# Sums of mm2's products gathered in one bank, some elementwise work on other engines, loads by single pages, and a new list of steps

## The chip, the cores and the metric

The kernel runs on one core of a Trainium2 chip. The metric is the device time of one execution in microseconds (us); the median of three runs of the kernel before is 296.47 us (296.28 to 297.04). PE is TensorE (its matmuls; PEld its weight loads), DVE is VectorE, ACT is ScalarE, POOL is GpSimd, SP is the engine that issues most DMAs.

## What is computed

The reference is a decayed linear attention followed by a two-layer MLP:

```python
batch, n_heads, seq, head_dim = (8, 8, 576, 64)
scores = scale * q @ k.T                      # per batch and head
gamma = 1.0 - 2.0 ** (-5.0 - np.arange(H))
Dmat = np.where(rel >= 0, gamma ** rel, 0.0)  # rel = row - column
x = ((scores * Dmat) @ v).transpose(0, 2, 1, 3).reshape(B * S, H * D)   # 4608 x 512
h = x @ w_in                                  # 512 x 2048
g = 0.5 * h * (1.0 + np.tanh(c * (h + 0.044715 * h * h * h)))
out = g @ w_out                               # 2048 x 512, float32
```

## The kernel before

The work of the attention is cut into 40 units, five per batch: four of 128 rows and a tail of 64. The decay is put into q and v (a product with a table, `dec` or `decw`), so that inside a unit a 0/1 mask is enough, and a running state (the sum of k^T v, two half-steps per unit) carries what lies before. Four pairs of units at the start (0 and 1, 2 and 3, 5 and 6, 7 and 8) are done as "wide" units of 256 rows. The MLP runs over nine blocks of 512 tokens: mm1 (x @ w_in), gelu, mm2 (g @ w_out). From block 1 on, mm2 is done per pair of 128-token tiles with seven products in place of eight: both operands are cut into 2x2 blocks, sums of blocks are formed on both sides, and the results are assembled from the seven products. For mm1 the same is done in the blocks 6 to 8.

Nothing is scheduled by the chip or by a planner at build time. The string `ORDER` is a list of steps written out by hand, and each engine gets its instructions in the order of this list. A step has a letter, its indices, and often the engine (`a` ACT, `g` POOL, `v` DVE):

- `L,u,n` loads q, k or v (n = 0, 1, 2) of unit u on SP; `I,g` and `J,g` load an eighth of w_in or w_out, by DMAs that POOL issues
- `q`, `k`, `v`: multiply or cast the loaded page to fp16; `t`/`D`: transpose by PE or DMA; `y`: copy a transpose out of its bank
- `X`, `Y,u,part`, `R` (wide units) and `B,u,w`: the matmuls of state, scores and result; `m`: the mask (L691, or L644 for wide units); `a`: add to the state (L711, L713); `o`: decay of the state; `z`: state to fp16; `x`: result to xT
- `N,t,f,half` and `M,t,f`: mm1 for two rows of 128 outputs and half of a block's tokens, or for one row and all tokens (L757); `F`, `G`: its gelu (L765); `O,t,n`: mm2 of block 0 (L783); `K,n`: n filler matmuls on the identity (L1003)
- `T` and `H,t,pr,i`: sums of blocks of w_out and of gelu's result (`tsum`, `ssum`, L817); `W,t,pr,i`: product i of mm2 (L860), eight matmuls of 256 columns; `V,t,pr,i`: the i-th step of assembly (L267, L269 or L817)
- `U` and `s,t,i`: sums of blocks of w_in and of x (they lie in the space of the tile `pages`); `A`, `l`, `f`: products (L957), assembly and gelu of mm1 in blocks 6 to 8
- `S`, `Q`: store

The products of mm2 go to two banks per pair, taken from a ring of two. Before, bank 0 is taken at product 1 and bank 1 at product 6. Products 1 and 2 share the left half of bank 0, 7 and 4 its right half, 6 has the left half of bank 1, 5 and 3 share the right one. Assembly copies product 1, adds product 6 and later sums in SBUF tiles `u1` to `u3`, and writes the blocks of `ost`, with five adds on DVE and two copies per pair.

The tile `pages` holds 21 pages of 256 KB for loads. Before, unit u takes three pages together, by u modulo 7 (modulo 3 from unit 31 on, when nine pages are left and the rest holds the sums `U` and `s`).

Of the kernel before, what the change touches and what calls it, by code (L numbers as in the profile page):

```python
# [17 lines left out]
L,0,1 Z,1,v L,0,0 I,2,g L,0,2 L,2,1 L,2,0 Z,2,g q,0 k,0,g I,7,g K,4 K,4 K,4 K,3 K,4 t,0,q,h L,2,2  # L18
L,4,1 c t,0,k,h I,1,g v,0,v X,0 y,0,k,v I,0,g I,3,g a,0,1 y,0,q,v Z,3,v k,2,g K,4 K,1 Y,0,1 t,2,k,o
m,0,1 z,0,1,a I,6,g K,4 Y,0,0 a,1,1 q,2 L,4,0 K,4 t,2,q,h m,0,0 y,2,k,a y,2,q,v I,4,g K,1 R,0 I,5,g  # L20
x,0 Y,2,1 L,5,0 x,1 i,4,v K,3 N,0,2,0 N,0,0,0 g o,1,1 m,2,1 L,5,1 Z,4,g v,2,v F,0,2,0 N,0,12,0 Y,2,0
F,0,0,0 z,1,1,v N,0,4,0 L,5,2 X,2 k,4,g Z,5,v q,4 F,0,12,0 F,0,4,0 t,4,k,o a,2,1 t,4,q,o a,3,1
y,4,q,a N,0,8,0 L,4,2 z,2,1,g L,9,1 N,0,10,0 F,0,8,0 k,5,g m,2,0 L,7,1 R,2 F,0,10,0 y,4,k,v B,4,-1
q,5 x,3 x,2 N,0,14,0 L,7,0 t,5,q,o N,0,0,1 L,7,2 J,1,g F,0,14,0 N,0,6,0 y,5,q,v J,3,g t,5,k,o
F,0,0,1 m,4 j,1,v J,0,g L,9,0 v,5,v J,2,g L,9,2 F,0,6,0 N,0,8,1 L,10,0 N,0,12,1 k,7,v X,5 y,5,k,a
F,0,8,1 z,3,1,g F,0,12,1 v,4,v Y,5,0 a,5,1 m,5,0 a,6,1 N,0,4,1 N,0,6,1 F,0,4,1 q,7 F,0,6,1 t,7,k,o
y,7,k,a N,0,2,1 J,5,g J,4,g N,0,14,1 F,0,2,1 J,6,g L,10,2 B,-1,4 F,0,14,1 x,4 Y,5,1 t,7,q,h y,7,q,a
J,7,g m,5,1 N,0,10,1 v,7,v F,0,10,1 z,5,1,g R,5 x,5 Y,7,0 o,6,1 x,6 O,0,0 O,0,4 q,10,g L,11,1
N,1,4,0 O,0,5 N,1,14,0 F,1,4,0 m,7,0 N,1,2,0 L,12,2 O,0,1 X,7 Y,7,1 F,1,14,0 F,1,2,0 L,15,1 k,9,a
O,0,6 O,0,2 N,1,10,0 F,1,10,0 q,9,g O,0,3 L,11,2 N,1,6,0 D,9 F,1,6,0 m,7,1 Z,0,g k,11,a a,7,1 O,0,7  # L30
e,0,0,v a,8,1 z,6,1,v O,0,12 T,1,0,v N,1,0,0 e,0,1,a F,1,0,0 z,8,1,g z,7,1,v N,1,8,0 O,0,13 L,10,1
N,1,12,0 R,7 B,9,-1 H,1,0,3,v v,10,v F,1,8,0 x,8 O,0,8 L,11,0 L,12,1 O,0,14 j,5,v F,1,12,0 v,11,v
T,1,1,v q,11 k,10,g x,7 O,0,15 N,1,6,1 H,1,0,1,v L,12,0 D,10 N,1,8,1 O,0,9 F,1,6,1 T,2,0,v v,9,v
O,0,10 e,0,3,a T,3,0,v S,0,0 N,1,14,1 F,1,8,1 H,1,0,2,v m,9 L,14,1 B,10,9 k,12,a D,11 T,2,1,v O,0,11
a,10,0 a,10,1 e,0,2,v N,1,12,1 L,13,2 F,1,14,1 L,13,0 x,9 N,1,10,1 m,10 F,1,12,1 T,3,1,v z,10,0,g
B,11,10 q,12,g W,1,0,1 S,0,3 v,13,v a,11,0 V,1,0,0,a a,11,1 x,10 v,12,v W,1,0,6 L,14,0 F,1,10,1
N,1,2,1 o,11,1 q,13,g F,1,2,1 T,4,0,v D,12 W,1,0,2 L,16,1 V,1,0,1,v N,1,4,1 N,1,0,1 S,0,2 V,1,0,2,a
z,11,0,v F,1,4,1 z,10,1,g j,2,v m,11 S,0,1 N,2,0,0 B,12,11 q,14 a,12,0 H,1,0,4,v k,15,g F,1,0,1
F,2,0,0 W,1,0,7 L,15,0 L,14,2 N,2,8,0 T,4,1,v N,2,4,0 V,1,0,3,v H,1,1,1,v L,13,1 z,12,0,g x,11
k,16,g H,1,1,2,v W,1,0,4 W,1,0,5 F,2,8,0 L,17,0 a,12,1 N,2,6,0 L,17,1 V,1,0,5,v L,19,0 F,2,4,0  # L40
k,13,g D,13 V,1,0,4,v F,2,6,0 m,12 N,2,14,0 v,14,v F,2,14,0 W,1,1,1 z,11,1,g V,1,1,0,a W,1,0,3
V,1,0,6,v L,16,0 N,2,10,0 F,2,10,0 k,14,g W,1,1,6 V,1,1,1,v N,2,12,0 z,12,1,v L,16,2 B,13,12 x,12
L,15,2 v,15,g D,14 q,15 W,1,1,2 H,1,1,3,v m,13 N,2,2,1 V,1,1,2,a W,1,1,7 F,2,12,0 N,2,2,0 V,1,1,3,v
k,17,a W,1,1,4 W,1,1,5 a,13,0 a,13,1 S,1,0 z,13,0,a q,19 q,17 q,16 F,2,2,1 S,1,1 D,15 L,17,2 F,2,2,0
L,18,0 N,2,8,1 B,14,13 N,2,12,1 L,20,0 F,2,8,1 V,1,1,5,v F,2,12,1 N,2,6,1 V,1,1,4,v W,2,0,1 x,13
N,2,10,1 F,2,6,1 m,14 H,2,0,1,v H,2,0,2,v z,13,1,v N,2,0,1 D,16 V,2,0,0,a L,24,1 B,15,14 H,1,1,4,v
a,15,0 L,18,2 H,2,0,3,v W,1,1,3 a,15,1 F,2,0,1 m,15 V,1,1,6,v q,18,g v,17,v F,2,10,1 N,2,4,1
N,2,14,1 L,18,1 L,19,1 x,14 v,16,g F,2,14,1 W,2,0,2 z,15,0,g B,16,15 W,2,0,6 F,2,4,1 x,15 k,19,g
a,16,0 N,3,8,0 V,2,0,1,v V,2,0,2,a a,16,1 F,3,8,0 o,16,1 z,16,0,v m,16 W,2,0,7 D,17 V,2,0,3,v L,23,1
v,18,g N,3,10,0 k,18,g F,3,10,0 L,24,0 L,20,1 N,3,4,0 F,3,4,0 z,15,1,g W,2,0,4 z,16,1,v B,17,16  # L50
L,21,0 N,3,0,0 q,20 V,2,0,5,v a,17,0 L,25,1 L,19,2 D,18 H,2,0,4,v L,20,2 S,1,2 W,2,0,5 N,3,12,0
W,2,1,1 F,3,0,0 m,17 q,21,g H,2,1,3,v V,2,0,4,v H,2,1,1,v F,3,12,0 k,20,g W,2,0,3 N,3,14,0 N,3,6,0
# [24 lines left out]
H,5,0,3,v N,5,12,0 L,34,1 W,4,1,6 N,5,2,1 F,5,12,0 N,5,8,1 k,32,a F,5,2,1 H,4,1,4,v q,32,g x,27
V,4,1,1,v W,4,1,2 N,5,4,1 H,5,0,1,v D,30 F,5,8,1 F,5,4,1 N,5,0,1 v,30,g z,28,1,g m,28 V,4,1,2,a
N,5,12,1 F,5,12,1 F,5,0,1 B,29,28 U,4,1 x,28 W,4,1,7 m,29 S,3,3 N,5,10,1 N,5,14,1 v,31,g D,31
B,30,29 L,34,0 L,33,0 U,4,0 V,4,1,3,v F,5,10,1 a,30,0 U,3,0 x,29 a,30,1 z,30,0,g i,3,a m,30 W,4,1,4  # L80
H,5,0,2,v N,5,6,1 W,4,1,5 V,4,1,4,v V,4,1,5,v F,5,14,1 B,31,30 z,30,1,g F,5,6,1 x,30 k,34,v i,5,a
W,4,1,3 a,31,0 W,5,0,1 m,31 V,5,0,0,a s,6,1 V,4,1,6,v S,4,1 a,31,1 A,6,0,1 s,6,2 s,6,3 A,6,0,2
l,6,0,0,a L,32,2 l,6,0,3,v W,5,0,6 A,6,0,6 q,33,g H,5,1,1,v W,5,0,2 o,31,1 L,33,1 l,6,0,1,a i,0,a
q,34 v,32,g A,6,0,7 s,6,4 D,32 z,31,0,g A,6,0,5 B,32,31 l,6,0,2,a V,5,0,2,a A,6,0,4 x,31 L,33,2
L,35,0 j,4,a W,5,0,7 l,6,0,4,v k,33,g f,6,0,0 L,35,2 D,33 A,6,0,3 V,5,0,1,v H,5,0,4,v a,32,0 v,33,g
a,32,1 f,6,0,1 A,6,1,1 l,6,1,0,a W,5,0,5 l,6,0,5,v f,6,0,2 m,32 A,6,1,6 V,5,0,3,v z,32,1,g z,31,1,a
L,35,1 l,6,1,1,v L,34,2 A,6,1,2 l,6,1,3,v z,32,0,v W,5,0,4 V,5,0,4,v D,34 V,5,0,5,v A,6,1,7
l,6,1,2,a f,6,0,3 A,6,1,5 B,33,32 L,36,0 q,35,g v,35,v L,36,1 l,6,1,4,v S,4,3 A,6,1,4 W,5,0,3
# [38 lines left out]
def kernel(  # L127
# [50 lines left out]

    def raw_of(u):
        return u % NR if u < LATE else (u - LATE) % 3  # L180

# [891 lines left out]
```

## Time and profile before

| | |
|---|---|
| runs | 296.28, 296.47, 297.04 us, median 296.47 |
| the profiled execution | 295.65 us, of which the span from the first to the last instruction is 293.9 |
| granted clock of TensorE | 1.000 |
| matmuls | 4064 |
| DMA | 49.79 MB, 169 GB/s in the mean; HBM read 36.70 MB, written 9.44 MB |
| DVE, ssum of 128x1024 (60) | 782 to 798 ns in the mean |
| DVE, add of 128x256 from a bank (75) | 415 ns |
| DVE, mask of 128x512 (24) | 684 ns |
| ACT, copy of 128x256 from a bank (30) | 371 to 374 ns |
| POOL, product of 128x512 fp32 (33) | 1115 to 1202 ns |

The profile lists busy time per engine, the span in 40 slices (each digit is a busy share in tenths), the chain of work that ended last (followed back from the last instruction), and groups of instructions as "line engine operation out<-in, shape, count | busy us, mean ns of one | idle time before, and what ended it". In the waits, the three numbers are us in total, times, and the longest. Matmuls are pipelined: the 273 ns of a 128x256 matmul is its length from start to end, while one follows the other after 0.109 us. In a table of stretches the pairs after the limits are the busy us of PE, PEld, DVE, ACT and POOL with the number of instructions, then the granted clock, the share of DMA and GB/s.

### The profile page before, as it was taken

The numbers are of one execution on the slowest core, as the hardware profiler recorded it, in microseconds if no ns is written. First come the engines' busy times: TensorE is split into PE (matmuls) and PEld (weight loads), VectorE is DVE, ScalarE is ACT, GpSimd is POOL, SyncE is SP. The second block draws the span as 40 slices with busy tenths as digits, with TensorE's granted clock in tenths as the row PEclk, the third lists the DMA queues.
The fourth block names the chain that finished last, engine by engine and source line by source line (L and its number), as shares of the span: only waits on it lengthen the run. The fifth ranks groups of instructions, "written<-read, shape, count | busy, mean of one in ns | idle before, by whom it ended". The sixth has DMA issues, their size and how long they took to land.

```text
span 293.9 us, 9639 instructions
## 1 busy us (share of the span) xinstructions
PE 280.3 (95%) x4064; PEld 235.2 (80%) x4064; DVE 216.6 (74%) x447; ACT 150.1 (51%) x289; POOL 109.6 (37%) x168
## 2 busy tenths in 40 slices
PE   3797999999999999999999999999999999999995
PEld 1355886667888888888888888888888788888874
DVE  7686753696865678576678699799889988977740
ACT  2144774334634543554553646546777587665411
POOL 5931910414351084163415544783467123000000
PEclk9999999999999999999999999999999999999999
DMA  7999999997979999989099978899498370002103
GB/s 212 283 236 250 217 220 211 214 179 162 248 142 228 178 186 220 230 206 210 23 235 214 196 166 178 187 204 153 131 195 208 75 205 7 36 8 102 74 25 121
DMA packets 136428, 49.79 MB, mean 169 GB/s; under 512 B 118208, under 2 KB 130880, under 8 KB 136384
## 3 DMA queue, kind: packets, MB, share of 16 engines
q1 hardware_dynamic: 132032, 44.97, 71.3%
q0 software_dynamic: 4352, 4.20, 8.5%
q8 instruction: 32, 0.52, 0.8%
q14 instruction: 12, 0.10, 0.1%
HBM read 36.70 MB, written 9.44 MB: 157 GB/s over the span
## 4 chain that ended last, share of the span: by engine, by line
PE 86%; POOL 5%; DMA 4%; DVE 3%; issue 1%; ACT 0%; POOLq 0%; ACTq 0%
PE bank L860 30%; PE bank L757 27%; PE bank L957 12%; PE bank L783 6%; DMA w_in_sb<-in_moe_w_in_dram 4%; PE sk L553 2%; PE x L529 2%; POOL w_in_sb L238 2%; PE sk L563 1%; PE x L574 1%; PE bank L987 1%; DVE pages L817 1%; POOL wide L269 1%; PE bank L493 1%; PE x L677 1%
## 5 line engine op out<-in xcount | busy, mean ns | idle before, releaser
L757 PE MATMUL bank<-xT,w_in_sb 128*128 128x256 f16 x768 | 94.4, 273 | 2.1 <-DMA w_in_sb<-in_moe_w_in_dram 2.1
L765 ACT ACTIVATE gT<-bank 128x512 f16<-128x512 f32 x96 | 56.7, 598 | 61.5 <-PE bank L757 59.7
L757 PEld LDWEIGHTS <-w_in_sb 128*128 128x128 f16 x768 | 73.8, 98 | 13.7 <-DMA w_in_sb<-in_moe_w_in_dram 2.7
L860 PEld LDWEIGHTS <-ssum 128*128 128x128 f16 x480 | 46.3, 98 | 6.5 <-issue 0.8
L269 POOL CAST sz<-s 64x256 f16<-64x256 f32 x48 | 24.4, 509 | 66.2 <-DVE s L713 45.9
L860 PE MATMUL bank<-tsum,ssum 128*128 128x256 f16 x360 | 46.0, 273 | 0.6 <-DVE ost L817 0.6
L860 PEld LDWEIGHTS <-gT 128*128 128x128 f16 x360 | 34.8, 98 | 4.5 <-issue 0.2
L424 POOL TENSOR_TENSOR qk<-pages,dec 128x512 f16<-128x512 f32 (+1 forms) x20 | 22.2, 1122 | 32.9 <-DMA pages<-in_q_dram 17.2
L860 PE MATMUL bank<-w_out_sb,gT 128*128 128x256 f16 x240 | 31.1, 273 | 0.0
L817 DVE TENSOR_TENSOR ssum<-gT 128x1024 f16<-128x1024 f16 x30 | 23.9, 798 | 3.9 <-ACT gT L765 3.5
L424 POOL TENSOR_TENSOR v<-pages,dec 128x512 f16<-128x512 f32 (+1 forms) x20 | 20.6, 1030 | 15.3 <-DMA pages<-in_v_dram 10.4
L817 DVE TENSOR_TENSOR ost<-u,bank 128x256 f32<-128x256 f32 x45 | 18.1, 416 | 9.5 <-PE bank L860 9.4
L817 DVE TENSOR_TENSOR ssum<-gT,ssum 128x1024 f16<-128x1024 f16 x30 | 23.4, 782 | 0.2
L691 DVE TENSOR_TENSOR ret<-sk,mask 128x512 f16<-128x512 f32 (+1 forms) x32 | 19.8, 618 | 4.3 <-PE sk L563 4.0
L957 PEld LDWEIGHTS <-pages 128*128 128x128 f16 x192 | 18.4, 98 | 2.8 <-issue 0.3
L957 PE MATMUL bank<-pages 128*128 128x256 f16 x144 | 20.3, 273 | 0.3 <-ACT pages L267 0.3
L783 PE MATMUL bank<-w_out_sb,gT 128*128 128x512 f16 x80 | 19.1, 380 | 0.0
L817 DVE TENSOR_TENSOR u<-u,bank 128x256 f32<-128x256 f32 x30 | 12.4, 415 | 8.7 <-PE bank L860 5.0
L713 DVE TENSOR_TENSOR s<-s,sk 128x256 f32<-128x256 f32 x36 | 14.9, 415 | 5.0 <-PE sk L563 4.0
L593 ACT ACTIVATE xT<-x 128x512 f16<-128x512 f32 (+1 forms) x25 | 14.3, 578 | 8.0 <-PE x L574 8.0
L817 DVE TENSOR_TENSOR hc<-hc,bank 128x512 f32<-128x512 f32 x21 | 14.4, 684 | 5.0 <-PE bank L957 2.3
L267 ACT COPY hc<-bank 128x512 f32<-128x512 f32 x19 | 11.1, 585 | 12.5 <-PE bank L957 12.4
(114 smaller groups left out, 425.8 us busy)
## 6 DMA issues: line engine op xcount, KB each, us to landing
out_dram<-ost SPq DMA_DIRECT2D x35, 256.0 KB, 3.4
pages<-in_q_dram SPq DMA_DIRECT2D x32, 256.0 KB, 4.7
pages<-in_v_dram SPq DMA_DIRECT2D x24, 256.0 KB, 4.1
pages<-in_k_dram SPq DMA_DIRECT2D x24, 256.0 KB, 4.3
pages<-in_k_dram SPq DMA_DIRECT2D x4, 512.0 KB, 5.2
pages<-in_v_dram SPq DMA_DIRECT2D x4, 512.0 KB, 6.0
w_in_sb<-in_moe_w_in_dram POOLq DMA_DIRECT2D x8, 256.0 KB, 9.8
w_out_sb<-in_moe_w_out_dram POOLq DMA_DIRECT2D x8, 256.0 KB, 10.6
```

What stands on the lines that cost most here:

```text
L267: nc.scalar.copy(out=o, in_=i)
L269: (nc.vector if eng == "v" else nc.gpsimd).tensor_copy(out=o, in_=i)
L424: eng.tensor_tensor(out=out, in0=s["raw"][:, i, 0:n], in1=dec[:, i // 2, s["j"], 0:n].unsqueeze(2).to_broadcast([128, n, D]), op=ALU.mult,)
L593: nc.scalar.activation(out=xT[:, :, o : o + G * (b - a)].rearrange("c p (h s) -> c p h s", s=G), in_=x[:, a:b].rearrange("c h p s -> c p h ...
L691: nc.vector.tensor_tensor(out=ret[:, :, 0:n], in0=now["two"][:, :, 0, 0:n], in1=mask.unsqueeze(1).unsqueeze(1).to_broadcast([128, 2, n, G] ...
L713: nc.vector.tensor_tensor(out=s32, in0=state[0], in1=kv, op=ALU.add)
L757: nc.tensor.matmul(hps[:, i, :], w_in_sb[:, ct, 128 * (fc + i) : 128 * (fc + i) + 128], xT[:, ct, TB * t % XR + lo : TB * t % XR + hi], st ...
L765: nc.scalar.activation(out=gTs[t][:, fc : fc + TB // (hi - lo), lo:hi], in_=h.pop((t, fc, lo)), func=AF.Gelu_apprx_tanh, bias=0.0, scale=1.0,)
L783: nc.tensor.matmul(ops[t, tcc], gTs[t][:, ft, 128 * tcc : 128 * tcc + 128], w_out_sb[:, ft, :], start=(ft == 0), stop=(ft == NFC - 1),)
L817: (nc.vector if eng == "v" else nc.gpsimd).tensor_tensor(out=out, in0=a, in1=b, op=op)
L860: nc.tensor.matmul(p["ps", bank][:, HN * col : HN * col + HN], a[:, k], b[:, k], start=(k == 0 and i in (1, 6)), stop=(k == HK - 1), skip_ ...
L957: nc.tensor.matmul(p["ps", bank][:, n], w[:, c, 128 * n : 128 * n + 128], x[:, c], start=(n == 0 and c == 0 and i in (1, 2, 5)), stop=(c = ...
```

## The change

1. **Products of mm2.** Products 1, 6, 7 and 4 now go to the left half of bank 0, one after the other onto the same sums, product 2 to the left half of bank 1, and 5 and 3 to its right half. Between them the running sum is copied out (four copies, on ACT or DVE), and three adds on DVE make the other blocks.
2. **Masks.** A form `m,u,h` has ACT copy the scores out of the bank to fp16 and POOL multiply them by the mask; 12 of 32 masks take it.
3. **State sums.** A form `a,u,half,g` has ACT copy the bank and POOL add it to the state; 15 adds take it, and one further first copy goes to ACT.
4. **Sums of operands.** `H`, `T`, `U` and `s` may name POOL: 23 of 60 `H`, 6 of 8 `T`, 1 of 8 `U` and 6 of 12 `s` do.
5. **Pages.** Each load takes single pages (two for a wide one) from a list of free ones; a page is put back at its last read.
6. **The list.** `ORDER` is new throughout. Four of block 0's mm1 steps are in the form of 512 columns (`M,0,8` to `M,0,11`), and there are 34 fillers for 36.

```diff
-    def raw_of(u):
-        return u % NR if u < LATE else (u - LATE) % 3
+    free = [12, 13, 14] + list(range(12)) + list(range(15, 3 * NR))
+    page_of, sums_on = {}, [False]
+
+    def page(u, n, width=1):
+        top = 9 if u >= LATE or sums_on[0] else 3 * NR
+        at = {p: i for i, p in enumerate(free) if p < top}
+        p = min(
+            (p for p in at if p + width - 1 in at), key=lambda p: (max(at[p], at[p + width - 1]), p)
+        )
+        for i in range(width):
+            free.remove(p + i)
+        page_of[u, n] = p
+        return p
+
+    def read(u, n, width=1):
+        free.extend(range(page_of[u, n], page_of[u, n] + width))
...
     def masked(u, *part):
...
+        if part:
+            if "two" in now:
+                nc.scalar.copy(out=ret[:, :, 0:n], in_=now["two"][:, :, 0, 0:n])
...
+            nc.gpsimd.tensor_tensor(
+                out=ret[:, :, 0:n], in0=ret[:, :, 0:n],
+                in1=mask.unsqueeze(1).unsqueeze(1).to_broadcast([128, 2, n, G]), op=ALU.mult,
+            )
...
-    def state_sum(u, half):
+    def state_sum(u, half, eng="v"):
...
-            nc.vector.tensor_copy(out=s32, in_=kv)
+            copy_on("a" if eng == "g" else eng, s32, kv)
+        elif eng == "g":
+            nc.scalar.copy(out=s32, in_=kv)
+            nc.gpsimd.tensor_tensor(out=s32, in0=state[0], in1=s32, op=ALU.add)
...
     def product(t, pr, i):
...
-            1: (blk_a(t, pr, 0, 0), blk_b(0, 0), 0, 0), 2: (blk_a(t, pr, 0, 1), blk_b(1, 0), 0, 0),
-            3: (s[3], blk_b(1, 1), 1, 1), 4: (blk_a(t, pr, 1, 1), tsum[3], 0, 1),
-            5: (s[0], tsum[0], 1, 1), 6: (s[1], tsum[1], 1, 0), 7: (s[2], tsum[2], 0, 1),
+            1: (blk_a(t, pr, 0, 0), blk_b(0, 0), 0, 0), 2: (blk_a(t, pr, 0, 1), blk_b(1, 0), 1, 0),
+            3: (s[3], blk_b(1, 1), 1, 1), 4: (blk_a(t, pr, 1, 1), tsum[3], 0, 0),
+            5: (s[0], tsum[0], 1, 1), 6: (s[1], tsum[1], 0, 0), 7: (s[2], tsum[2], 0, 0),
         }[i]
+        fresh = ("ps", bank) not in p
+        if fresh:
+            p["ps", bank] = take("o")
...
-                start=(k == 0 and i in (1, 6)), stop=(k == HK - 1), skip_group_check=True,
+                start=(k == 0 and fresh), stop=(k == HK - 1), skip_group_check=True,
...
     def assemble(t, pr, i, eng):
...
+        if i in (0, 1, 3):
+            copy_on(eng, part_of(t, pr, (1, 2, 0, 3)[i]), ps(0, 0))
+        elif i == 5:
+            copy_on(eng, block_c(t, pr, 1, 0), ps(0, 0))
         elif i == 2:
+            combine("v", block_c(t, pr, 0, 0), part_of(t, pr, 1), ps(1, 0), ALU.add)
         elif i == 4:
+            combine("v", block_c(t, pr, 1, 1), part_of(t, pr, 3), ps(1, 1), ALU.add)
         else:
+            combine("v", block_c(t, pr, 0, 1), part_of(t, pr, 2), ps(1, 1), ALU.add)
...
-    def sum_w(i, part):
+    def sum_w(i, part, eng="v"):
...
-    def sum_x(t, i):
+    def sum_x(t, i, eng="v"):
```

The first lines of the list, before and after, and a stretch of the new one near block 7:

```diff
-L,0,1 Z,1,v L,0,0 I,2,g L,0,2 L,2,1 L,2,0 Z,2,g q,0 k,0,g I,7,g K,4 K,4 K,4 K,3 K,4 t,0,q,h L,2,2
-L,4,1 c t,0,k,h I,1,g v,0,v X,0 y,0,k,v I,0,g I,3,g a,0,1 y,0,q,v Z,3,v k,2,g K,4 K,1 Y,0,1 t,2,k,o
+L,0,1 Z,1,v Z,5,v L,2,0 L,0,0 L,4,1 I,1,g q,0 k,0,g K,4 K,4 K,4 K,4 K,3 t,0,q,h t,0,k,h L,0,2
+y,0,q,v y,0,k,a Z,3,v q,2,g I,0,g K,4 K,1 Y,0,0 Z,4,g L,4,0 t,2,q,o L,2,1 k,4,a y,2,q,a v,0,g
+t,4,k,o X,0 m,0,0 I,7,g I,6,g I,2,g a,0,1 K,2 Y,0,1 g a,1,1 q,4,g m,0,1 k,2,a z,0,1,a L,2,2 K,4 K,1
...
+H,6,0,1,v f,6,3,2 A,7,0,1 W,6,0,1 V,5,1,6,v L,39,0 L,38,0 s,7,1,g l,6,3,5,v l,7,0,0,a a,36,0
+V,6,0,0,a s,7,2,g A,7,0,6 L,38,2 m,36 l,7,0,1,a s,7,3,g L,39,2 W,6,0,5 A,7,0,2 L,38,1 A,7,0,7
```

More of the change, by code (lines that the diff above doesn't have):

```diff
@@ L23 @@
[L23 to L28, printed above, removed]
@@ L194, in load_wide @@
         i = slice(128 * c, 128 * c + 256)
+        page(u, n, 2)
         r = wide_page(u, n)
@@ L428, in times @@
         )
+        read(s["u"], i)
     def half16(s, name):
@@ L684, in masked @@
     def masked(u, *part):
-        if part:
+        if part and part[0] != "h":
             return wide_masked(u, *part)
@@ L917 @@
     w_in_g = w_in_sb.rearrange("p c (g i f) -> p c g i f", g=4, i=2)
-    def sum_w(i, part):
+    def sum_w(i, part, eng="v"):
+        if not sums_on[0]:
+            assert all(p in free for p in range(9, 3 * NR))
+            sums_on[0] = True
         g = slice(2 * part, 2 * part + 2)
```

247 lines of the change are left out of this document (121 added, 126 removed).

## The prediction

> **What bounds the kernel now.** I read the busy line first, then the slices, then the chain that ended last.
>
> ```profile
> PE 280.3 (95%) x4064; PEld 235.2 (80%) x4064; DVE 216.6 (74%) x447; ACT 150.1 (51%) x289; POOL 109.6 (37%) x168
> PE   3797999999999999999999999999999999999995
> PEclk9999999999999999999999999999999999999999
> DMA  7999999997979999989099978899498370002103
> PE 86%; POOL 5%; DMA 4%; DVE 3%; issue 1%; ACT 0%; POOLq 0%; ACTq 0%
> ```
>
> PE is busy in every slice from the fifth (about 29 us) to the last, at full clock; the chain is 86% PE. A change that leaves PE's work alone can only gain where PE waits. Those places are in the waits of PE:
>
> ```profile
> PE bank L1003 <- DVE ident L364: 4.5, 1, 4.5
> PE bank L757 <- DMA w_in_sb<-in_moe_w_in_dram: 2.1, 2, 1.6
> PE bank L1003 <- DVE qkT L269: 1.9, 1, 1.9
> PE bank L860 <- DVE ost L817: 0.6, 1, 0.6
> PE sk L636 <- DVE qkT L269: 0.5, 1, 0.5
> PE bank L957 <- DVE pages L817: 0.4, 1, 0.4
> PE bank L957 <- ACT pages L267: 0.3, 1, 0.3
> ```
>
> The first is the setup, which the change does not touch. Before 31 us there are 4.5 us of others, after it only 1.3 us in this view. The matmuls' start times in the trace give some more for the late part, since a wait also shows as an interval over the usual 0.109 us between two 128x256 matmuls (16 take 1.75 us in the chain): 0.80 us extra at 227.7, 0.58 at 225.0, 0.46 at 253.2, 0.19 at 278.2, 0.13 at 224.0, in all 2.2 us. So at most 4.5 + 2.2 = 6.7 us can be gained, and any amount lost. Why DVE is late there is seen in the stretches (columns: PE, PEld, DVE, ACT, POOL):
>
> ```profile
> 200.00:220.00 20.00, 20.00 (x346) 17.86 (x345) 17.22 (x37) 14.54 (x29) 9.54 (x14) 1.00 0.76 155
> 220.00:240.00 20.00, 18.95 (x265) 16.45 (x263) 19.32 (x37) 13.57 (x28) 8.45 (x11) 1.00 0.68 159
> 240.00:260.00 20.00, 19.71 (x263) 17.41 (x262) 16.49 (x34) 14.04 (x30) 2.27 (x3) 1.00 0.11 41
> ```
>
> DVE is full (19.32 of 20) only where PE falls to 18.95.
>
> **PE's own work.** The instruction order of the new kernel has the same PE work with two filler matmuls fewer (34 for 36, 0.216 us apart: -0.43 us) and 16 products of 512 columns in place of 32 of 256 (16 x 0.216 = 3.45 us by the L783 piece of the chain, against 32 x 0.109 = 3.50). That is -0.5 us at most, and nothing where the filler stood before a wait.
>
> **Start, to about 44 us.** Both lists need some 12 us of PE work before the first mm1 step and 31 to 32 us before the first mm2 step (steps of the list times the matmuls' intervals), which now ran at 21.3 and 44.3 us: 12 us of these 44 were lost to waits, setup and half-rate filler. The new list takes the copy of unit 0's kT off DVE (there two copies of 0.69 and 1.22 us in a row, and PE's wait of 1.9 us) to ACT (1.01 us), beside DVE: about -1 us. It puts the multiplications of q2, v0 and v2 (128x1024) on POOL. No row has them: POOL takes 0.61 us for 256 elements and 1.04 for 512 (shortest of L424), a line that gives 1.9 for 1024; DVE takes 1.22. As POOL issues w_in's loads in order, I0 goes out at about 11.3 us (11.9 before), but I6 and I7 stand behind v0, at 14 to 15.5 (I7 at 9.0 and I6 at 14.3 before). The load that PE waited for landed 10.5 us after its issue, so the third mm1 step waits again until 25 or 26 us (24.85 before). What is late next is w_in, as now; DMA is busy in nearly every slice up to 60 us. I take -0.6 us for the start, fillers in it. Bounds: -3 (two of three early waits gone) to +1.5: w_out's loads J1 onward stand on POOL behind a mask, a state sum and v4, some 3 us later than the 30.05 us of now, and J1 plus 10.6 us is 43.6, where the list wants it at 42.
>
> Loading page by page frees a page at its last read, not a unit's three together. SP issues the same loads; its waits for pages in the trace (8.7 us for v L424 the longest) are in front of loads that PE never waited for. I take nothing. If loads run further ahead, they share DMA with w_out; that is in the +1.5.
>
> **The middle and the end.** Counted in the two orders, times the mean of the row of each:
> - mm2's sums: DVE loses 30 adds of 0.415 us (-12.5) and gains 29 copies of 0.42 (+12.2); ACT has 31 copies for 30. Even.
> - 12 masks: DVE loses 8 x 0.684 + 4 x 0.42 = 7.2 us; ACT gains 12 copies (6.2), POOL 12 products (8 x 1.04 + 4 x 0.61 = 10.8).
> - state sums: 15 adds and a copy leave DVE (-6.6); ACT gains 16 copies of 0.37 (5.9), POOL 15 adds of 128x256 (0.61 by the nearest row: 9.2).
> - operand sums: 30 of 128x1024 (23 ssum, 6 tsum, 1 of w_in) and 6 of 128x512 leave DVE (about -27); POOL takes 30 x 1.9 + 6 x 1.04 = 63 us. Bounds for the 1.9: 1.04 (a row for half the size) and 3.0 (twice the 1.5 of a POOL product held up).
> - other casts and products change engine: about +9 on DVE, -13 on POOL.
>
> DVE: -32 us, to some 185. ACT: +19, to 169. POOL: +65, to 175 of 294. No engine reaches PE's total. By stretches of the list of 20 us of PE work each, DVE's counted sum (scaled by 0.93, since instructions overlap: 234 counted, 217 in the page) is 20.5 and 20.4 us at 200 to 240 now; after, 18.3, 20.8, 19.2, 16.0 from 160 to 240. So DVE is full for one stretch instead of two. I take half of the 2.2 us: -1.1. Bounds -2.2 and the rivals below.
>
> New waits. Now no half of a bank takes more than two products, and in a pair three products wait for a copy or add (2, 4, 3); after, 1, 6, 7 and 4 share one half, and four wait (6, 7, 4, 3). The loop of such a wait is shown near the end of now, in the chain and in the timeline:
>
> ```profile
> 278.00 0.44 PE bank L957 x4
> 278.44 0.02 issue
> 278.46 3.65 PE bank L860 x32
> ```
>
> ```profile
> 278.04 0.37 ACT L267 COPY u<-bank 128x256 f32<-128x256 f32 x1 [0.28 <-PE bank L860]
> ```
>
> Product 1 of the last pair ended at 278.00, its copy ran to 278.41, product 2 began at 278.46: a loop of 0.46 us. The new list puts at least 0.87 us of other PE work into each such gap, 12 times just that (7 times now); the cover is gone if the copying engine is over 0.4 us late. I take zero, bound 12 x 0.4 = +4.8; below zero nothing, a wait is added. Behind the waiting matmul stand all later steps of PE.
>
> Sums on POOL: what waits for them is a product or, for one operand, the next sum on DVE. Most have 3 to 17 us of PE work between sum and product in the list; 5,0 has 1.7 us, 7,1 has 1.3. A sum in block 7 of x (s,7,1 and s,7,2) must start after product 5 of the group before and both end before product 6: 2 x 1.04 us in 3.1 us of PE work. Zero taken.
>
> The end is as before: last the 128 columns of the last tile (0.27 us on ACT), then 64 KB out.
>
> **Sum.** -0.6 - 1.1 = -1.7 us. From the profiled execution (295.65 us; span 293.9) that is 293.95; the runs' median is 296.47, 0.8 over that execution, so the forecast is 294.8 us, -0.6%.
>
> **Rivals.**
> 1. *Slower: DVE and POOL hold each other up.* In the trace:
>
> ```profile
> 225.63 1.50 POOL L424 TENSOR_TENSOR qk<-pages,dec 128x512 f16<-128x512 f32 x1 [0.89 <-DMA pages<-in_q_dram]
> 226.25 1.42 DVE L817 TENSOR_TENSOR ssum<-gT,ssum 128x1024 f16<-128x1024 f16 x1
> 217.83 0.68 DVE L817 TENSOR_TENSOR ssum<-gT 128x1024 f16<-128x1024 f16 x1
> ```
>
> A DVE sum that takes 0.68 us alone takes 1.42 beside a POOL product, and that one 1.50 for 1.04. From 160 to 240 of the new list there are 13 sums on POOL and 26 on DVE. If each POOL sum delays DVE by half its 1.9 us, that is 12 us where DVE has 5 free (79.4 us of PE work less 74.3 of DVE's): 7 us late, and PE with it. Price +4 (what PE's steps in between don't hide) to +6: 296.47 - 0.6 + 4 to 6 = 300 to 302 us. It decides from 5 us of added DVE time in this stretch. For it: DVE's casts and sums in the profile spread by a factor of two. Against: DVE has fewer such sums left to be blocked, 26 there for 38 now.
> The Trainium skill ("SBUF — State Buffer", section "Who interferes with whom") has the rule: a DVE instruction with two SBUF inputs and a POOL instruction that reads SBUF share a port pair as an exclusive lock, held for the whole instruction, so the longer POOL sum blocks longer. By that rule, the trace agrees: 1.42 for 0.68.
> 2. *Given back in the bank.* The 12 tight gaps cost 0.19 us each, as the one at 278.2 did, 2.3 us: 297.1, no change. For it: the copies queue behind DVE instructions of 0.69 us. Against: all waits of L860 for a copy or an add now make 0.6 us in the waits of PE and that 0.19.
> 3. *Hidden by the loads.* The start at +1.5 instead of -0.6: 296.9.
> 4. *All waits before and after 31 us go*: -3 - 2.2 = 291.3.
>
> That the change doesn't do what it says is excluded by the orders: 23 ssum are gone from DVE.
>
> **Chances.** Forecast (293.5 to 295.5) 0.44; rival 4 0.07; rivals 2 and 3 together 0.18; rival 1 0.31, a third of it as a milder loss of 1 to 3 us. About 0.3%, or 0.9 us, is what a measurement of this kernel can tell from no change. Faster 0.50, same 0.16, slower 0.34. The range leaves out half of rival 4 and the worst of rival 1: 292.0 to 300.0; the forecast's own is 293.5 to 295.5.
>
> **What would show it.** Right: PE stays 9 in all slices after the start, the steady part starts by 31 us, DVE falls to about 185 us, no POOL line among PE's waits. Wrong: waits of PE or of DVE for POOL's ssum or pages; ssum on DVE with a mean over 0.9 us (rival 1); waits of L891 on copies of bank (2); waits on w_in or w_out past 26 us (3). A POOL sum far over 1.9 us would make the count wrong.

## The result, and the profile after

The new kernel takes 321.45 us (median of four runs, 320.48 to 322.86) and the kernel before 296.38 us beside it: a ratio of 1.0845, 95% interval 1.0801 to 1.0889. The change makes the kernel slower by 25 us. The forecast was 294.8 us in a range of 292.0 to 300.0; it was wrong in sign and far outside the range. The mechanism of rival 1 came, at some five times its price.

The profiled execution took 322.86 us, the longest of the four, with a span of 321.2 us. These are the busy line and the slices of its page, which answer to those of before:

```profile
PE 288.2 (90%) x4046; PEld 236.2 (74%) x4046; DVE 232.8 (72%) x404; ACT 166.6 (52%) x332; POOL 186.7 (58%) x195
PE   4897999999988898998999999958988889889996
DVE  6673663997459649548874999998988997886540
PEclk9997999999999799999999999998999999999999
PE 17%; DVE 6%; issue 1%; ACT 0%; DVEq 0%; ACTq 0%
```

PE was 9 in every slice from the fifth to the last but one. Now it falls to 8 and once to 5, first in the twelfth slice (88 us) and then again and again to the end. DVE has 43 instructions fewer than before (404 for 447) and is busy for 16 us more. The chain's shares add up to only 24%, so here it carries no reading. The waits of PE do, in the order of the view:

```profile
PE bank L1034 <- DVE ident L378: 4.5, 1, 4.5
PE bank L891 <- DVE u L283: 4.3, 4, 1.5
PE x L547 <- DVE sz L283: 3.6, 3, 2.3
PE sk L571 <- DVE v L438: 2.6, 1, 2.6
PE bank L988 <- DVE pages L847: 2.6, 2, 1.4
PE bank L787 <- DMA w_in_sb<-in_moe_w_in_dram: 2.2, 2, 1.8
PE bank L891 <- DVE ost L847: 1.7, 2, 1.5
PE sk L571 <- DVE ret L719: 1.5, 2, 1.0
```

The first is the setup, as before. All the others of these lines but the load of w_in name DVE (ACT and POOL are named further down, for 0.8 us and less): PE waits for copies, casts, products and masks of DVE, in every part of the kernel behind 60 us, and not for the sums that the change put on POOL. Two stretches answer to those shown of before (same columns):

```profile
200.00:220.00 20.00, 16.56 (x268) 13.97 (x267) 18.93 (x29) 10.00 (x23) 11.24 (x10) 0.91 0.59 135
240.00:260.00 20.00, 15.10 (x180) 12.62 (x180) 17.95 (x26) 10.10 (x20) 12.84 (x14) 1.00 0.42 73
```

In the first, DVE had 37 instructions in 17.22 us before (0.47 us each); now 29 take 18.93 us (0.65 each). They are not the same steps, since the new kernel is later by then; the groups of instructions say which became longer (out<-in, shapes, count, busy us and mean ns of one):

```profile
L847 DVE TENSOR_TENSOR ssum<-gT 128x1024 f16<-128x1024 f16 x21 | 23.8, 1142 | 0.5 <-ACT gT L795 0.4
L847 DVE TENSOR_TENSOR ost<-u,bank 128x256 f32<-128x256 f32 x45 | 18.3, 413 | 17.8 <-PE bank L891 13.9
L283 DVE CAST sz<-s 64x256 f16<-64x256 f32 x32 | 20.6, 645 | 2.0 <-POOL s L741 1.7
L847 POOL TENSOR_TENSOR ssum<-gT,ssum 128x1024 f16<-128x1024 f16 x14 | 30.4, 2170 | 20.1 <-DVE ssum L847 19.8
```

DVE's sum of two operands in SBUF (the memory of the tiles, to which the banks do not belong) takes 1142 ns in the mean, for 798 before. Its add with one operand in a bank has not changed (413, was 415). The cast of the state takes 645 ns, and the shortest of its kind in the trace 275 (before, the 16 of them on DVE took 290 in the mean). One place in the timeline shows how (start, duration, engine, line):

```profile
211.46 2.30 POOL L847 TENSOR_TENSOR ssum<-gT,ssum 128x1024 f16<-128x1024 f16 x1
211.71 2.60 DVE L438 TENSOR_TENSOR v<-pages,dec 128x512 f16<-128x512 f32 x1
214.23 0.68 DVE L847 TENSOR_TENSOR pages<-w_in_sb 128x1024 f16<-128x1024 f16 x1
214.36 0.32 PE L571 MATMUL sk<-v,qk 64*64 64x64 f16 x16 [2.63 <-DVE v L438]
```

A product that takes DVE 0.68 us elsewhere starts 0.25 us after a POOL sum, ends 0.55 us after it, and has then taken 2.60 us. PE waited 2.63 us for it. Nobody waited for the POOL sum. The Trainium skill ("SBUF — State Buffer", section "Who interferes with whom") says that whichever of the two engines issues first gets the shared ports for its whole instruction and the other blocks; this place agrees, 2.60 us for 0.68.

A measure of this over a whole kernel is used below, under the name **lengthening**: each DVE instruction's duration less the shortest of the same form (operation, names, shapes, and for copies out of a bank the strides) in that kernel, summed over all. It is 18.9 us before and 60.0 us after (40.5 in instructions with two operands in SBUF, 17.6 in casts; 1.9 in all others). DVE's work without it went from 197.7 to 172.8 us. The intervals between PE's matmuls beyond 0.28 us, less 0.11 us each, sum to 10.9 us before and 33.4 after; up to 40 us they are 8.4 and 7.3, and all the growth lies behind 60 us. The span grew by 27.3 us: these intervals make 22.5 of them, and three stretches at half the granted clock at most another 5.1 (the last section has one of them).

### The profile page after: what moved, and what is told of

It reads as the page before. It is cut to its first block, busy times and chain, and to the rows that moved or that the text cites. A ratio compares the mean times of both kernels' runs of the same rounds, so it can differ in the third digit from the quotient of the medians.

```text
span 321.2 us, 9622 instructions
## 1 busy us (share of the span) xinstructions
PE 288.2 (90%) x4046; PEld 236.2 (74%) x4046; DVE 232.8 (72%) x404; ACT 166.6 (52%) x332; POOL 186.7 (58%) x195
## 5 line engine op out<-in xcount | busy, mean ns | idle before, releaser
L787 PE MATMUL bank<-xT,w_in_sb 128*128 128x256 f16 (+1 forms) x752 | 97.7, 280 | 2.7 <-DMA w_in_sb<-in_moe_w_in_dram 2.2
L847 POOL TENSOR_TENSOR ssum<-gT,ssum 128x1024 f16<-128x1024 f16 x14 | 30.4, 2170 | 20.1 <-DVE ssum L847 19.8
L714 POOL TENSOR_TENSOR ret<-ret,mask 128x512 f16<-128x512 f16 (+1 forms) x12 | 13.5, 1121 | 21.7 <-ACT ret L710 18.4
L988 PE MATMUL bank<-pages 128*128 128x256 f16 x144 | 21.6, 276 | 3.3 <-DVE pages L847 1.2
L847 DVE TENSOR_TENSOR ssum<-gT 128x1024 f16<-128x1024 f16 x21 | 23.8, 1142 | 0.5 <-ACT gT L795 0.4
L741 POOL TENSOR_TENSOR s<-s,s 128x256 f32<-128x256 f32 x12 | 9.4, 781 | 25.4 <-ACT s L740 21.1
L283 DVE CAST sz<-s 64x256 f16<-64x256 f32 x32 | 20.6, 645 | 2.0 <-POOL s L741 1.7
L847 POOL TENSOR_TENSOR ssum<-gT 128x1024 f16<-128x1024 f16 x9 | 20.4, 2271 | 0.9 <-ACT gT L795 0.8
L438 POOL TENSOR_TENSOR qk<-pages,dec 128x512 f16<-128x512 f32 (+1 forms) x19 | 20.2, 1066 | 1.1 <-PE bank L988 0.9
L611 ACT ACTIVATE xT<-x 128x512 f16<-128x512 f32 (+1 forms) x25 | 14.5, 586 | 10.3 <-PE x L592 10.3
L847 DVE TENSOR_TENSOR ssum<-gT,ssum 128x1024 f16<-128x1024 f16 x16 | 17.4, 1088 | 1.8 <-POOL ssum L847 1.7
L438 POOL TENSOR_TENSOR v<-pages,dec 128x512 f16<-128x512 f32 (+1 forms) x15 | 16.4, 1091 | 3.5 <-PE x L592 1.7
```

The costliest lines, as they stand in the source:

```text
L283: (nc.vector if eng == "v" else nc.gpsimd).tensor_copy(out=o, in_=i)
L438: eng.tensor_tensor(out=out, in0=pages[:, page_of[s["u"], i], 0:n], in1=dec[:, i // 2, s["j"], 0:n].unsqueeze(2).to_broadcast([128, n, D]) ...
L611: nc.scalar.activation(out=xT[:, :, o : o + G * (b - a)].rearrange("c p (h s) -> c p h s", s=G), in_=x[:, a:b].rearrange("c h p s -> c p h ...
L714: nc.gpsimd.tensor_tensor(out=ret[:, :, 0:n], in0=ret[:, :, 0:n], in1=mask.unsqueeze(1).unsqueeze(1).to_broadcast([128, 2, n, G]), op=ALU. ...
L741: nc.gpsimd.tensor_tensor(out=s32, in0=state[0], in1=s32, op=ALU.add)
L787: nc.tensor.matmul(hps[:, i, :], w_in_sb[:, ct, 128 * (fc + i) : 128 * (fc + i) + 128], xT[:, ct, TB * t % XR + lo : TB * t % XR + hi], st ...
```

## The experiments

The theory after the result: POOL's reads of SBUF hold DVE up, DVE's steps come late, and PE waits for single steps of DVE although DVE is idle a quarter of the time. Rivals: POOL's own slowness (a sum of 2.1 us where DVE takes 0.8), the four products in one half bank, the new list.

### Taking parts of the change back

**a_sums_dve**: the new kernel with all `H`, `T`, `U` and `s` on DVE.

```diff
-H,1,0,1,g
+H,1,0,1,v
...
-T,3,0,g
+T,3,0,v
```

> The changed kernel with all sums of operands (H, T, U, s) back on DVE, the rest as changed. Theory 1, POOL's reads hold up DVE: the 36 sums (73 us of POOL time) are the largest part of what holds DVE, so DVE's lengthening (60 us over the shortest of each form, 19 before) falls to 30 to 40 us although 36 instructions come back, and the time to 303 to 310 us. Theory 2, the new list and the four products in one bank stall PE by themselves: 316 to 322 us. Theory 3, masks and state sums over ACT and POOL are too late for PE: 314 to 320 us.

Measured 306.54 us, ratio to before 1.0351 (1.0323 to 1.038); lengthening 26.5 us, PE's intervals 21.1. DVE's busy time fell by 13 us (219.4 for 232.8) although 36 sums came back to it.

**a_mask_state_dve**: 12 masks and 15 state sums back on DVE.

```diff
-m,4,h
+m,4
...
-a,5,1,g
+a,5,1
```

> The changed kernel with the 12 masks and 15 state sums back on DVE, the operand sums still on POOL. Theory 1: POOL reads 22 us less, DVE is given 14 us more to do, so 314 to 320 us. Theory 2: 316 to 322 us. Theory 3: 300 to 308 us, PE's waits for sz and for the state's products go.

Measured 315.82 us, 1.0668 (1.0631 to 1.0705); lengthening 47.4 us.

**a_both_dve**: both edits together.

> The changed kernel with sums, masks and state sums all on DVE: what is left is the products in one bank, the loads by pages and the new list. Theory 1: DVE's lengthening near the 19 us of before, 296 to 302 us (the list was not made for these engines, so not all comes back). Theory 2: 312 to 322 us.

Measured 303.52 us, 1.0261 (1.022 to 1.0303); lengthening 12.6 us, PE's intervals 17.0. So of the loss of 25 us, 15 go when the sums alone leave POOL, 5 to 6 when masks and state sums alone do, and 18 when both do; some 7 us stay.

### Putting parts into the kernel before

**b_sums_pool**: 23 `H` and 6 `T` of the old list on POOL, as in the new list, nothing else.

```diff
-H,1,0,1,v
+H,1,0,1,g
```

> The kernel before, with 29 sums (23 H, 6 T, the same ones as in the changed kernel) on POOL, nothing else: its list, its banks, its masks. Theory 1: most of the loss comes with this part alone, 306 to 318 us, DVE's lengthening 40 us or more. Theory 2: 295 to 300 us.

Measured 309.47 us, 1.0447 (1.0411 to 1.0484). Lengthening 40.0 us for 18.9. This one part alone makes the old kernel 13 us slower, and DVE, which lost 29 sums, is busier than before (221.9 us for 216.6). PE also waits once, for 3.3 us, for a cast on POOL, so this run alone does not tell the hold-up of DVE from a late POOL.

**b_extra_read** and **b_extra_write** tell POOL's slowness from the hold-up. In the old kernel every step stays where it is; behind each of the same 29 sums, which DVE still does, POOL gets an instruction that nobody needs: once an add that reads 768 columns of w_out twice, once two memsets that only write.

```diff
+    def extra():
+        w = w_out_sb.rearrange("p c f -> p (c f)")
+        nc.gpsimd.tensor_tensor(
+            out=spare.bitcast(F16), in0=w[:, 0:768], in1=w[:, 768:1536], op=ALU.add
+        )
...
+        for _ in range(2):
+            nc.gpsimd.memset(spare.bitcast(F16), 0.0)
```

> The kernel before, all its own work where it was, with 29 additional sums on POOL that read 128x768 of w_out and write a spare tile that nobody reads; each stands in the list where one of the 29 sums stood that went to POOL in b_sums_pool. Theory 1 (POOL's reads hold up DVE): about 1.6 us of POOL time each, 46 us in all, three quarters of the 61 us of b_sums_pool, DVE's lengthening rises from 19 to 30 us or more and the time to 300 to 308 us, although nothing waits for these sums. Theory 3 (POOL is late as a producer): only POOL's own later casts move, 297 to 301 us, with DVE's lengthening near 19 us.

> As b_extra_read, but with 58 memsets of 128x768 on POOL (two for each sum, together about as long), which read nothing. Theory 1: DVE's two-operand sums keep their time, lengthening 19 to 23 us, and the time is 296 to 299 us. If only the occupied queue of POOL counted, as theory 3 has it, it would be as slow as b_extra_read.

Measured 311.93 us for the reads, 1.0488 (1.0435 to 1.054), and 297.12 us for the writes, 1.0023 (1.0005 to 1.0041). First the busy line and the group of the extra instruction with reads, then a place in its timeline:

```profile
PE 286.9 (92%) x4064; PEld 238.2 (77%) x4064; DVE 240.9 (77%) x447; ACT 150.5 (48%) x289; POOL 162.4 (52%) x197
L979 POOL TENSOR_TENSOR spare<-w_out_sb 128x768 f16<-128x768 f16 x29 | 51.6, 1779 | 1.1
```

```profile
64.19 6.06 POOL L979 TENSOR_TENSOR spare<-w_out_sb 128x768 f16<-128x768 f16 x3
64.58 2.12 DVE L421 TENSOR_TENSOR v<-pages,dec 128x512 f16<-128x512 f32 x1
66.63 2.12 DVE L814 TENSOR_TENSOR tsum<-w_out_sb 128x1024 f16<-128x1024 f16 x1
68.68 2.12 DVE L421 TENSOR_TENSOR qk<-pages,dec 128x512 f16<-128x512 f32 x1
73.92 0.42 PE L550 MATMUL sk<-v,qk 64*64 64x64 f16 x16 [4.56 <-DVE ret L688]
```

The same for the writes:

```profile
PE 281.7 (95%) x4064; PEld 235.5 (80%) x4064; DVE 217.5 (74%) x447; ACT 150.2 (51%) x289; POOL 152.6 (52%) x226
L979 POOL MEMSET spare<- 128x768 f16 x58 | 43.1, 743 | 2.5
```

DVE has the same 447 instructions in both. With the reads it is busy for 23 us more (240.9), with the writes it stays at 217.5 (lengthening 43.3 and 19.3 us). Three POOL adds in a row force three DVE instructions of 0.68 us into their own rhythm, 2.12 us each, and PE waits 4.56 us for a mask behind them in DVE's queue. The useless work occupies POOL for 51.6 us in one and 43.1 in the other. So occupying POOL is not what costs; its reads of SBUF are. The same section of the Trainium skill says that a DVE instruction with two SBUF inputs contends with a GpSimd instruction that reads SBUF, not with one that only writes it: 311.9 to 297.1 us agrees.

**b_z_act**: less POOL work in the old kernel, 13 casts of the state moved to ACT.

```diff
-z,25,0,g
+z,25,0,a
```

> The kernel before with 13 casts of the state to fp16 (z, units 25 and later) moved from POOL to ACT, the opposite direction of the change: POOL reads SBUF 13 us less between 160 and 245 us, ACT has 10 us more. Theory 1: DVE's lengthening falls from 19 to about 15 us, and of PE's 2.2 us of waits in the late part 0.5 to 1.5 go: 295 to 296 us. Against it: ACT's queue delays gelu and copies: 296.5 to 299 us.

Measured 298.41 us, 1.006 (1.0039 to 1.0081): no gain, but 2 us lost. Lengthening fell to 17.6 us, less than expected. PE has a new wait of 1.5 us for one of these casts on ACT, so this says only that a cast moved to another queue can be late there too.

**b_mask_state**: the 12 masks and 15 state sums of the new list in the old one, with one first copy that goes to ACT with them; **b_state**: the state sums and this copy without the masks.

```diff
-a,5,1
+a,5,1,g
...
-m,4
+m,4,h
```

> The kernel before with 12 masks and 15 state sums moved to ACT and POOL alone. Theory of POOL's reads: 27 more POOL instructions that read SBUF, some 24 us, lengthen DVE's instructions with two operands in SBUF; by the 13 us that 58 us of POOL's operand sums cost, that is 5 us, less what 14 us less work on DVE gives back: 299 to 302 us, DVE's lengthening over 25 us (18.9 before). Rival: the work comes off a full DVE and POOL has time: 295 to 296.5 us.

> The kernel before with the 15 state sums (and one first copy) alone on ACT and POOL, masks on DVE. If the state's path is what costs (each state passes ACT's copy, POOL's sum and POOL's cast in turn before a product may start): 307 to 315 us, with waits of x on sz from POOL of 4 us or more. If the masks cost: 297 to 300 us.

Measured 317.8 us, 1.071 (1.0669 to 1.0752), and 311.0 us, 1.0504 (1.0465 to 1.0543). The first was expected near 300, so the reads were the wrong reason here: lengthening is only 22.5 and 23.1 us. The waits of b_state show another (line and releaser, us in total, times, longest), which makes 7.8 of the 12.0 us by which PE's intervals grew there (22.9 for 10.9); a place of it shows the path:

```profile
PE x L525 <- POOL sz L265: 7.8, 5, 2.6
```

```profile
148.98 0.37 ACT L718 COPY s<-sk 128x256 f32<-128x256 f32 x1
149.43 0.72 POOL L719 TENSOR_TENSOR s<-s,s 128x256 f32<-128x256 f32 x1 [4.01 <-ACT s L718]
150.09 0.85 POOL L265 CAST sz<-s 64x256 f16<-64x256 f32 x2
151.00 0.29 PE L525 MATMUL x<-qkT,sz 128*128 128x64 f16 x4 [2.43 <-POOL sz L265]
```

The state is a chain through all units, and DVE does its add in 0.41 us. By ACT and POOL it is 0.37 + 0.72, and the cast stands behind it: 2.0 us from the copy's start to PE's. In this place of the old list no PE work covers that: PE waits 2.43 us. What the masks add, some 6 us, was not taken apart. In the new list this path is not among PE's larger waits (one of 0.8 us for sz from POOL; the longest wait for sz from DVE, 2.3 us, stands behind a sum of 2.29 us and a cast of 2.20 us in DVE's queue). Taking masks and state sums back took 12.6 us of lengthening with them. Both point to the hold-up as what they cost in the new list; no run there parted it from the state's path.

### What stays: products, list, pages

**b_products** put the new products and their assembly alone into the old list; some copies stand there behind the next product, so that blocks of `out` from block 1 on hold other sums than the reference's. **b_products2** has seven steps moved so that each copy stands ahead of the next product. The first pair of lines is of both, the rest of b_products2 alone:

```diff
-V,1,0,5,v
+V,1,0,5,a
...
+V,2,1,1,v
...
-V,2,1,1,v
```

> The kernel before with the products' part of the change alone: products 1, 6, 7, 4 onto one half of a bank with copies between, in the old list (of the copies, steps 0 and 5 on ACT, 1 and 3 on DVE, so that the counts per engine stay 75 on DVE and 30 on ACT). If the 7 us that remain in a_both_dve come from the waits in the bank: 300 to 304 us, with waits of PE's product line on ost or u. If they come from the new list: 296 to 298.5 us.

> The kernel before with the new products and their assembly alone, seven steps of the old list moved so that each copy stands before the product that follows it onto the same sums. Chain theory: as in the run of the products before, 303 to 306 us, with waits of the product line on u and ost. List theory: the old list keeps its time, 296 to 298 us.

Measured 305.25 us, 1.0292 (1.0248 to 1.0335), and 306.42 us, 1.0344 (1.0292 to 1.0395). In the old list the chain of four costs 9 to 10 us, and PE's waits name it (b_products2):

```profile
PE bank L857 <- DVE u L265: 3.3, 6, 0.8
PE bank L857 <- DVE ost L813: 2.8, 3, 1.2
```

**a_short_chain** asks the same of the new list: a_both_dve with products 7 and 4 in the right half of bank 0, so that two products share a half, not four.

```diff
-4: (blk_a(t, pr, 1, 1), tsum[3], 0, 0)
+4: (blk_a(t, pr, 1, 1), tsum[3], 0, 1)
...
-7: (s[2], tsum[2], 0, 0)
+7: (s[2], tsum[2], 0, 1)
...
+        elif i == 3:
+            combine("v", part_of(t, pr, 3), part_of(t, pr, 2), ps(0, 1), ALU.add)
```

> The new kernel with masks, state sums and operand sums back on DVE (303.5 us in its own run), and products 7 and 4 moved from the left half of bank 0 to its right half: two products one after the other share a half in place of four, 14 copies become adds, nothing else differs and the list is the same. If the chain of four in one half is what is left of the loss (waits of the product line on u and ost): 298 to 300 us, and those waits below 1 us. If the new list or the single pages are: 303 to 304 us, with the waits elsewhere.

Measured 304.87 us, 1.0273 (1.0248 to 1.0298), against 1.0261 of a_both_dve: nothing given back. The edit is not clean, since 18 instructions move from ACT to DVE with it (DVE 226.2 us for 216.9). But in a_both_dve itself, with the chain of four, the product line waits for its copies only here:

```profile
PE bank L887 <- DVE u L279: 0.4, 1, 0.4
```

The new list was written round the four copies; what is left of the loss is not there.

**a_s_pool** (a_both_dve, but the six `s` and one `U` on POOL again), **a_all_back** (a_both_dve with every cast, product with the decay, copy and assembly of mm1 on the engine that the old list names) and **a_all_back_short** (that, with the short chain):

```diff
-s,6,4,v
+s,6,4,g
```

```diff
-q,2,g
+q,2
...
-k,4,a
+k,4,g
```

> The new kernel with masks, state sums and operand sums on DVE (303.5 us), but the six sums of blocks of x and the one of w_in left on POOL, as the new list has them. Theory of due times (the list was written for these sums on POOL, and DVE comes to them too late): the waits of the products of x on the sums in pages (4.4 us) go, and the time falls to 299 to 301 us. Rival (the order or the other engines): 302 to 304 us, other waits in their place.

> The new kernel with every step on the engine that the old list names for it (masks, state sums, operand sums, casts, products of q and v with the decay, copies of transposes, assembly of mm1), the new order, the single pages and the new products kept. If the engines of the casts and products make the rest of the loss: 296 to 299 us. If the new order and the new products do: 303 us or more, since nothing in this order was written for these engines.

> The same with two products of mm2 in the shared half of the bank in place of four: order and pages alone are then new. Order theory: as a_all_back to within 1.5 us. Chain theory: 3 us or more below it.

Measured 305.42 us, 1.0334 (1.0275 to 1.0394); 309.75 us, 1.0455 (1.0401 to 1.0508); 312.02 us, 1.0518 (1.046 to 1.0576). None gives anything back. With the old engines the new order is slower still, and the short chain gains nothing there either. What these runs leave is the order itself, or the pages, though no wait of PE in them names a load of q, k or v; the pages had no run of their own.

**a_act_more**: a_both_dve with seven casts of the state (units 25 to 32) and ten copies of mm2's running sum moved from DVE to ACT.

```diff
-z,25,0,v
+z,25,0,a
...
-V,4,0,3,v
+V,4,0,3,a
```

> The new kernel with masks, state sums and operand sums on DVE (303.5 us), and seven casts of the state (units 25 to 32) and ten copies of the running sum of mm2's products (blocks 4 to 6) moved from DVE to ACT: some 8 us less on DVE from 164 to 240 us. If DVE is late there because the new order gives it too much at once: 299 to 301.5 us, the waits of PE on DVE's sums in pages shorter. If it is the order itself (what stands before what): 303 to 305 us.

Measured 304.39 us, 1.0259 (1.0216 to 1.0302): no gain, though DVE fell from 19.30 to 17.20 us in the stretch from 180 to 200. So less work on DVE there does not help. PE's longest wait stayed, and the timeline of a_both_dve shows who stands ahead of the add that it waits for:

```profile
198.66 1.35 DVE L843 TENSOR_TENSOR pages<-w_in_sb,pages 128x1024 f16<-128x1024 f16 x1
199.93 0.41 DVE L843 TENSOR_TENSOR pages<-xT,pages 128x512 f16<-128x512 f16 x1
200.26 0.68 DVE L843 TENSOR_TENSOR ssum<-gT,ssum 128x1024 f16<-128x1024 f16 x1
200.86 0.68 DVE L715 TENSOR_TENSOR ret<-sk,mask 128x512 f16<-128x512 f32 x1
201.47 0.67 DVE L843 TENSOR_TENSOR pages<-pages,bank 128x512 f32<-128x512 f32 x1
202.19 0.60 PE L984 MATMUL bank<-pages 128*128 128x256 f16 x4 [2.04 <-DVE pages L843]
```

**a_order** moves that add ahead of those four, and one sum of x at 229 us ahead of two others.

```diff
-A,6,0,2 B,32,31 ... U,4,1 L,35,0 A,6,0,7 W,5,0,2 s,6,4,v z,31,1,a H,5,0,2,v m,32 D,33 l,6,0,3,v
+A,6,0,2 l,6,0,3,v B,32,31 ... U,4,1 L,35,0 A,6,0,7 W,5,0,2 s,6,4,v z,31,1,a H,5,0,2,v m,32 D,33
...
-s,7,1,v l,6,3,5,v l,7,0,0,a a,36,0 V,6,0,0,a s,7,2,v
+s,7,1,v s,7,2,v l,6,3,5,v l,7,0,0,a a,36,0 V,6,0,0,a
```

> The new kernel with masks, state sums and operand sums on DVE (303.5 us), two steps of the list moved and nothing else: the add l,6,0,3 from behind a sum of w_in, a sum of x, a sum of operands and a mask to right behind its product, and the sum s,7,2 from behind an add and a state sum to right behind s,7,1. If the order of DVE's steps makes the last loss: the waits of 2 us at 200 and 228 us shrink or go, 299.5 to 301.5 us. If something else stands behind them: the waits stay or come a little later, 303 to 304 us.

Measured 302.69 us, 1.0199 (1.016 to 1.0238), against 1.0261 (1.022 to 1.0303): in the expected direction but smaller, and the intervals overlap. PE's waits on DVE's `pages` went from 4.4 to 2.4 us. Two steps of the order may thus explain 1 to 2 of the 7 us; that the other 5 are more of the same kind was not shown.

**b_y0k_act** tests the start: the old kernel with the copy of unit 0's kT on ACT.

```diff
-y,0,k,v
+y,0,k,a
```

> The kernel before with one step changed: the copy of unit 0's kT goes from DVE to ACT, as in the new list. If that copy sets the start, as the prediction has it: about 295.4 us, and the wait of 1.9 us on qkT goes. If the loads of w_in set it: 296.4 us and the wait is only named otherwise.

Measured 296.19 us, 0.9999 (0.9982 to 1.0016): nothing. PE still waits 1.7 us for `qkT` (1.9 before), so this copy does not set the start.

## Why the prediction was wrong, step by step

**The step that failed** is in the middle: "DVE: -32 us, to some 185", and from it "So DVE is full for one stretch instead of two ... -1.1". DVE measured 232.8 us. The work that was counted did leave in the main: without lengthening DVE does 25 us less. But lengthening rose by 41 us: the count, with the means of the old profile, held every remaining instruction at its old duration, and POOL's reads made them longer. The same paragraph's rows add up to +70 us for POOL, not +65, and those for ACT to +12.5, not +19; measured are +77 and +16.5. The forecast does not rest on these two.

**Rival 1 named this and priced one stretch of it.** It charged the 13 POOL sums between 160 and 240 us with half of 1.9 us each, 12 us, of which 7 were to reach PE. These 80 us are PE work counted along the list, not times of the trace: in the trace of the new kernel the 13 sums lie between 190.9 and 278.2 us, and the same matmuls of 256 columns, counted from the end, between 178.6 and 254.2 us before. There lengthening rose from 6.6 to 19.6 us, by 13.0, and PE's intervals from 1.8 to 12.1, by 10.2. The delay of DVE was thus priced nearly right, and more of it reached PE than was charged. That is luck in part, since masks and state sums on POOL, which were not charged, hold DVE up as well. What was left out is the list ahead of this stretch, where DVE had free time by the count. From 60 us to it lengthening rose from 9.4 to 34.2 us and PE's intervals from 0.2 to 10.3, with POOL busy for 87.2 us where it had been for 47.8; behind it PE's intervals rose from 0.2 to 3.4. PE waits for a particular step of DVE, and a step that is 2 us late makes PE late whether DVE idles before and after or not: the part ahead cost as much as the stretch that was priced, with DVE busy for 11.36 of 20 us in one piece of it (80 to 100). "Against: DVE has fewer such sums left to be blocked" was true and did not help, since casts and products with the decay are blocked as well.

**Sums on POOL.** The size was nearly right: 2.12 us for the shortest, 1.9 estimated, bounds 1.04 and 3.0. "Zero taken" for what waits for them held for PE; one sum of DVE waited 1.7 us for a sum of POOL.

**New waits in the bank.** Zero was taken, with a bound of +4.8 us. After, PE's waits on `u` and `ost` are 6.0 us; with POOL's new work undone (a_both_dve), 0.4 on `u`, and a shorter chain gave nothing. So these waits are the late DVE again: the cover of 0.87 us per gap is enough when DVE is in time. Without a list made for it the chain costs 9 to 10 us (b_products2).

**Start.** -0.6 us forecast; PE's intervals up to 40 us fell by 1.1. But the granted clock, 1.00 there before, was 0.53 from 28 to 30 us and 0.62 from 30 to 32, which takes the gain back: the matmuls still to be done at 40 us come to 256.2 us of PE work in both traces (an estimate, from the usual intervals of each form). And the reason given, the copy of kT, does nothing alone (b_y0k_act).

**PE's own work and pages.** No wait of PE names a load except that of w_in (2.2 us, was 2.1), so pages at nothing stands. PE's own work went the other way: the granted clock fell (below), and the profiled execution has 0.984 in the mean for 1.000.

**What would show it.** "ssum on DVE with a mean over 0.9 us (rival 1)" was the sign that came: 1142 ns.

Of the 25 us, then, about 18 are POOL's new work, and by the waits of PE nearly all of them come by the hold-up of DVE. Putting back the other engines or shortening the chain of four gave none of the other 7 back; moving two steps may have given back 1 to 2, and the rest is open.

## What to carry to other kernels

Before elementwise work goes from DVE to POOL, charge POOL's reading time with the hold-up of DVE's casts and two-operand instructions (here 0.34 to 0.53 us of DVE for each us more, over whole kernels: 21.1 for 62.3 in b_sums_pool, 24.4 for 52.8 in b_extra_read, 41.1 for 77.1 in the new kernel; in b_mask_state only 0.15, 3.6 for 23.5), in every stretch of the kernel, and don't set free time of DVE against it: what counts is how late the one step comes that PE waits for next. A shorter busy total on an engine says nothing if its instructions become longer; look at a group's mean beside its shortest. And a hand-written order is only as good as the durations that it was written for: its parts can't be judged by what they cost in another list.

## What the runs showed of the hardware that was not expected

- **A wait of PE can be paid twice.** After some waits the granted clock fell to half, with PE at work again. These are four stretches of 2 us of the new kernel, behind the wait of 2.63 us that ended at 214.36:

```profile
212.00:214.00 2.00, 0.00 (x0) 0.00 (x0) 2.00 (x1) 0.78 (x2) 1.76 (x1) 1.00 1.04 290
214.00:216.00 2.00, 1.64 (x58) 1.48 (x58) 2.00 (x6) 0.00 (x0) 0.00 (x0) 0.96 0.25 55
216.00:218.00 2.00, 2.00 (x11) 1.34 (x10) 2.00 (x4) 1.56 (x3) 1.06 (x1) 0.50 0.41 80
218.00:220.00 2.00, 2.00 (x14) 1.54 (x13) 1.27 (x3) 0.14 (x1) 2.00 (x3) 0.69 0.61 120
```

  From 216 to 218 us a matmul starts every 0.213 us, where a full clock has 0.109. Fifteen matmuls of this place took over 400 ns, for 273, and lost some 1.5 us. The trace has three such slow stretches of 3.41 us, from 28.1, 106.6 and 215.8 us, behind intervals between matmuls of 2.12, 2.49 and 2.82 us. The length of the wait alone does not decide: an interval of 1.91 us was followed by one in b_extra_read and one of 2.62 us in b_mask_state, but one of 2.62 us in a_short_chain and another in b_state were not. Where the wait lies does: the three starts are 23 and 32 times 3.413 us apart. The traces of 18 kernels (all but a_all_back and a_all_back_short), cut from 4.5 us on into windows of 3.413 us in step with their slow stretches, show it. After each of the 13 windows in which PE was idle for 0.549 or more of the time a slow one followed, after 3 of the 4 between 0.50 and 0.549, and after those below 0.50 only twice, where the clock was slow already. The wait of 2.62 us in b_mask_state left one window idle for 0.71, the one in b_state was split between two and left at most 0.44. The Trainium skill ("TensorE: Matmul & The Clock Gate", section "What's actually happening") has a gate that halves the clock after an idle window of about 3.4 us; the halving and the 3.41 us agree, and here a window idle for little more than half of it sufficed.
- POOL memsets of 0.74 us, 58 of them, left DVE's lengthening where it was (19.3 us for 18.9).
- DVE's casts from SBUF are held up as well: 645 ns in the mean for 275 at the shortest. Its adds with one operand in a bank kept their 413 ns.
